# Two stored spectra loaded earlier, the u rows moved to other tables, and the order lists of four engines written anew

## The chip, the cores and the metric

The kernel runs on one core of one Trainium2 chip. The metric is the device time of one execution in microseconds (us), as the median of several. Executions of one kernel here lie within about 3% of each other, and some fall into a slower state with a lower granted clock; those are named. Medians and ranges below are over all executions, ratios over the fast ones alone. The engines are TensorE (PE in the profile), VectorE (DVE), ScalarE (ACT), GpSimd (POOL) and the DMA engines, whose transfers are issued by SyncE (SP), ScalarE and GpSimd.

## The reference, cut to what matters

Two independent parts of 2048 x 448 outputs stand side by side. Part A is a linear attention with softmax features. Part B is a long convolution of a signal u with a kernel K that is itself a sum of 256 damped complex rotations for each of 448 channels:

```python
P = jnp.exp(logdA[:, :, None] * l[None, None, :])             # damped rotations
K = jnp.einsum("dn,dnl,dn->dl", Cc, P, dB).real               # kernel rows, 448 x 2048
Kf, Uf = rfft2(pad(K)), rfft2(pad(u))                         # spectra (calls cut)
y = irfft2(Uf * Kf)[..., :L] + u * Dskip                      # product of spectra, inverse, skip term
out = concatenate([attention(x), y], axis=-1)
```

## The kernel before: what the change touches

K is built in four quarters of the channels. For each quarter ScalarE evaluates two tables, rotations (Sin, lines 487 and 488) and dampings (Exp, line 496, with a negation in line 498). VectorE multiplies them (lines 534 and 535, then 539 to 542), and TensorE multiplies the low table W by the high table U (line 566) into kernel rows:

```python
def rotations(qt):                                   # T: Sin
    p = args(TH, ...)
    for e, n, f, rows_ in evals(2):
        act(T[:, 0, rows_, :], p[:, e:e + n], ACT.Sin, scale=float(f), bias=bias_hp[:, :])   # 487
        act(T[:, 1, rows_, :], p[:, e:e + n], ACT.Sin, scale=float(f))                       # 488
def dampings(qt):                                    # W: Exp
    ...
    act(W[:, c, ...], p[:, e:e + n], ACT.Exp, ...)                                           # 496
    act(W[:, c, 1:30:2, 1, :], W[:, c, 1:30:2, 0, :], ACT.Copy, scale=-1.0)                  # 498
def damp(qt, c):
    yield TT(out=w[:, 1:30:2], in0=w[:, 1:30:2], in1=t[:, 0:N_ABS - 1], op=ALU.mult)         # 534
    yield TT(out=w[:, 0:31:2], ...)                                                          # 535
    ...
```

A copy (line 570) takes the rows out of TensorE's banks, and a scatter (line 672) of 20 small DMAs turns them into the natural order. DFT tiles (line 681) and matmuls (line 696) then make a kernel spectrum for each of three column groups, which ScalarE evicts (line 699). The first group holds two quarters, called group 0 here; groups 1 and 2 are quarters 2 and 3.

```python
def scatter_k(gi, Ts, engs):
    for kt, h0, h1, l0, l1 in K_ROWS:
        for g in range(4):
            next(engs).dma_start(out=Kt[:, kt, ...], in_=Ts[32 * g + h0:32 * g + h1, l0:l1, :])   # 672
def load_su(gi):                                     # stored spectrum of u, from DRAM
    nc.gpsimd.dma_start(out=SU[gi]..., in_=SUd...[:, :, 112 * q0:112 * (q0 + nq)])                # 779
def conv_group(gi, SU, SK, UD, GI, OB):
    prod(...)      # VectorE: SU times SK, line 712; sums in 717 to 727
    inverse(...)   # UD times Dskip (729); TensorE: inverse DFT (738), skip term (740); eviction (745)
```

Nothing is left to a scheduler: four lists fix the order of all instructions of TensorE, ScalarE, VectorE and SyncE.

```python
def in_order(tc):
    for engine, name in (("PE", "PE"), ("ACT", "Activation"), ("DVE", "DVE"), ("SP", "SP")):
        places = ...decode(ORDER[engine])
        for a, b in zip(places, places[1:]):
            tc.add_manual_dep(queues[name][b], queues[name][a].name, info, reason="order")
```

In the program built from this, eight semaphores are shared in turn by the DMAs of SyncE and ScalarE, so that each such DMA waits for the eighth before it.

The softmax here doesn't subtract the row's maximum and nothing guards it: scores larger than these inputs give would overflow.

## Time and profile before

Three runs had a median of 339.19 us (334.77 to 339.36). The profiled execution took 335.67 us; the span between its first and last instruction is 333.9 us.

| stage (us from the start) | VectorE busy | VectorE idle | what ends the longest waits |
|---|---|---|---|
| 0 to 261.3: attention, tables, kernel rows | 233.2 | 28.1 | loads (first 20 us), ScalarE's tables (quarters 1 and 3) |
| 261.3 to 326.1: convolution | 57.0 | 7.8 | group 2's kernel spectrum, 6.2 |
| 326.1 to 333.9: last inverse and stores | 0 | 7.8 | |

The longest wait of the convolution, in VectorE's timeline (start, duration, what, idle before and its releaser):

```profile
312.26 3.96 DVE L712 TENSOR_TENSOR sbuf<-sbuf 128x3584 bf16<-128x3584 bf16 x2 [6.16 <-ACT sbuf L699]
```

The page also draws the span as 40 equal slices (8.35 us each), each digit the busy share of a slice in tenths. Two of its rows, before:

```profile
DVE  4689999899998999949799999999699999995590
DMA  7947000000001111014111213579821848510006
```

VectorE is at 90% and more nearly everywhere. The dips are the first two slices, the "4" and "7" at 142 to 167 us, the "6" at 234 us and the two fives before the end. The DMA engines are busy from 217 to 242 us ("798") and again during the last scatter (from 275 us, "85").

### The profile page before, as it was taken

The numbers are of one execution on the slowest core, as the hardware profiler recorded it, in microseconds if no ns is written. First come the engines' busy times: TensorE is split into PE (matmuls) and PEld (weight loads), VectorE is DVE, ScalarE is ACT, GpSimd is POOL, SyncE is SP. The second block draws the span as 40 slices with busy tenths as digits, with TensorE's granted clock in tenths as the row PEclk, the third lists the DMA queues.
The fourth block names the chain that finished last, engine by engine and source line by source line (L and its number), as shares of the span: only waits on it lengthen the run. The fifth ranks groups of instructions, "written<-read, shape, count | busy, mean of one in ns | idle before, by whom it ended". The sixth has DMA issues, their size and how long they took to land.

```text
span 333.9 us, 8889 instructions
## 1 busy us (share of the span) xinstructions
PE 248.6 (74%) x3735; PEld 180.1 (54%) x3735; DVE 290.2 (87%) x361; ACT 251.8 (75%) x539; POOL 10.3 (3%) x20
## 2 busy tenths in 40 slices
PE   2937858888738778999489987889449853599864
PEld 1914534444425445666256755567338742598854
DVE  4689999899998999949799999999699999995590
ACT  5899999999999999998669996899993310132411
POOL 3000000000000000000000000020000040000000
PEclk9987899999987997999589999999789795599979
DMA  7947000000001111014111213579821848510006
GB/s 218 272 117 224 22 1 0 29 0 27 3 0 69 47 52 57 19 47 129 35 43 57 71 59 75 163 259 306 254 54 31 295 118 155 166 62 2 2 2 220
DMA packets 32055, 31.42 MB, mean 94 GB/s; under 512 B 10448, under 2 KB 30704, under 8 KB 31632
## 3 DMA queue, kind: packets, MB, share of 16 engines
q1 hardware_dynamic: 28856, 25.42, 25.4%
q0 software_dynamic: 1296, 5.15, 5.8%
q8 instruction: 29, 0.48, 0.6%
q10 hardware_dynamic: 1864, 0.30, 0.5%
q14 instruction: 10, 0.08, 0.1%
HBM read 22.94 MB, written 7.34 MB: 91 GB/s over the span
## 4 chain that ended last, share of the span: by engine, by line
DVE 25%; PE 16%; ACT 12%; DMA 7%; issue 3%; SPq 1%; DVEq 0%; ACTq 0%
DMA sbuf<-sbuf 5%; DVE sbuf L540 3%; DVE sbuf L542 3%; ACT sbuf L496 3%; DVE sbuf L539 3%; DVE sbuf L642 3%; DVE sbuf L535 2%; PE bank_72 L696 2%; DVE sbuf L534 2%; DVE sbuf L712 2%; ACT sbuf L699 2%; PE bank_71 L696 2%; PE bank_65 L738 2%; DMA out_dram<-sbuf 2%; PE bank_66 L738 2%
## 5 line engine op out<-in xcount | busy, mean ns | idle before, releaser
L566 PEld LDWEIGHTS <-sbuf 128*16 128x16 bf16 x1792 | 36.9, 115 | 9.7 <-issue 7.5
L318 PE MATMUL bank_72<-sbuf 128*128 128x448 bf16 x128 | 32.7, 379 | 6.9 <-ACT sbuf L321 5.9
L738 PEld LDWEIGHTS <-sbuf 128*128 128x128 bf16 x384 | 28.5, 103 | 14.5 <-issue 13.3
L699 ACT CAST sbuf<-bank_72 128x448 bf16<-128x448 f32 x28 | 15.5, 553 | 27.5 <-DMA sbuf<-sbuf 15.2
L696 PEld LDWEIGHTS <-sbuf 128*128 128x128 bf16 x336 | 24.8, 108 | 20.0 <-issue 18.4
L696 PE MATMUL bank_72<-sbuf 128*128 128x112 bf16 (+1 forms) x256 | 25.3, 249 | 10.8 <-ACT sbuf L699 10.5
L712 DVE TENSOR_TENSOR sbuf<-sbuf 128x3584 bf16<-128x3584 bf16 (+1 forms) x9 | 23.6, 2643 | 6.3 <-ACT sbuf L699 6.2
L566 PE MATMUL bank_65<-sbuf 128*16 128x48 bf16 x896 | 23.0, 262 | 2.2 <-DVE sbuf L542 2.2
L566 PE MATMUL bank_66<-sbuf 128*16 128x48 bf16 x896 | 23.8, 262 | 0.2
L579 PEld LDWEIGHTS <-sbuf 112*128 112x128 bf16 x128 | 12.3, 98 | 19.8 <-issue 11.5
L321 ACT CAST sbuf<-bank_72 128x448 bf16<-128x448 f32 x32 | 18.5, 577 | 4.3 <-PE bank_72 L318 4.2
L534 DVE TENSOR_TENSOR sbuf<-sbuf 128x3360 bf16<-128x3360 bf16 x8 | 15.2, 1903 | 6.7 <-ACT sbuf L488 3.5
L318 PEld LDWEIGHTS <-sbuf 128*128 128x128 bf16 x128 | 12.0, 102 | 16.2 <-issue 10.2
L542 DVE TENSOR_TENSOR sbuf<-sbuf 128x896 bf16<-128x896 bf16 (+1 forms) x24 | 18.7, 779 | 0.7
L539 DVE TENSOR_TENSOR sbuf<-sbuf 128x896 bf16<-128x896 bf16 (+1 forms) x24 | 18.6, 777 | 0.4
L540 DVE TENSOR_TENSOR sbuf<-sbuf 128x896 bf16<-128x896 bf16 (+1 forms) x24 | 18.6, 775 | 0.3
L639 PEld LDWEIGHTS <-sbuf 112*128 112x128 bf16 x128 | 9.3, 102 | 16.5 <-issue 12.7
L496 ACT ACTIVATE sbuf<-bank_67 128x112 bf16<-128x112 f32 (+2 forms) x60 | 18.0, 412 | 0.0
L496 ACT ACTIVATE sbuf<-bank_68 128x112 bf16<-128x112 f32 (+2 forms) x60 | 18.0, 452 | 0.0
L586 DVE TENSOR_REDUCE sbuf<-sbuf 128x32 f32<-128x896 bf16 x16 | 17.3, 1081 | 0.4 <-ACT sbuf L582 0.3
L579 PE MATMUL bank_70<-sbuf 112*128 112x448 bf16 x64 | 14.7, 351 | 3.0 <-ACT sbuf L584 3.0
L522 DVE TENSOR_TENSOR sbuf<-sbuf 128x448 bf16<-128x448 bf16 (+3 forms) x16 | 16.5, 1030 | 0.2
(177 smaller groups left out, 653.0 us busy)
## 6 DMA issues: line engine op xcount, KB each, us to landing
sbuf<-const SPq DMA_DIRECT2D x32, 224.0 KB
SUd<-sbuf SPq DMA_DIRECT2D x16, 224.0 KB
sbuf<-const SPq DMA_DIRECT2D x2, 1024.0 KB
sbuf<-in_A_x_dram SPq DMA_DIRECT2D x4, 448.0 KB
out_dram<-sbuf SPq DMA_DIRECT2D x16, 112.0 KB
sbuf<-SUd POOLq DMA_DIRECT2D x1, 1792.0 KB, 13.3
sbuf<-in_B_u_dram SPq DMA_DIRECT2D x4, 448.0 KB
sbuf<-SUd POOLq DMA_DIRECT2D x2, 896.0 KB, 9.4
```

The source lines that it names most:

```text
L318: mm(p[:, 0:D_MODEL].rearrange("p (q g x) -> p q g x", q=4, g=4), lhsT=G1[:, cp, jt, 128 * mt:128 * mt + 128], rhs=by_quarter(ab[:, cp ^ s ...
L496: act(W[:, c, a:a + 2 * (rows_.stop - 1 - rows_.start) + 1:2 * rows_.step, 1 - neg, :], p[:, e:e + n], ACT.Exp, scale=float(f - 2 * f * neg))
L534: yield TT(out=w[:, 1:30:2], in0=w[:, 1:30:2], in1=t[:, 0:N_ABS - 1], op=ALU.mult)
L539: yield TT(out=t2, in0=flipped(src), in1=far[:, :, cols].unsqueeze(1).to_broadcast([128, n, 2, COLS]), op=ALU.mult)
L540: yield TT(out=dst, in0=src, in1=PW[512][:, 0, cols].unsqueeze(1).unsqueeze(1).to_broadcast([128, n, 2, COLS]), op=ALU.mult)
L542: yield TT(out=dst, in0=dst, in1=t2, op=ALU.add)
L566: mm(p[32 * g:32 * g + N_HI, qq * N_LO:(qq + 1) * N_LO], lhsT=U[qt % 2][:, c, :, ri, xc], rhs=W[:, c, :, ri, xc], start=(i == 0), stop=(i ...
L579: mm(p[:, :], lhsT=xT[:, dj, ts], rhs=w[:, dj, :], start=(dj == 0), stop=(dj == 3))
L696: mm(p[:, k2, :].rearrange("p (q g x) -> p q g x", q=nq, g=4), lhsT=f_tiles[i][1][:, fi, :], rhs=natural(Kt[:, kt, :] if kt < 5 else K0[:, ...
L699: nc.scalar.copy(SK[:, b, i0 // 8, i0 // 4 % 2, i0 % 4:i0 % 4 + per, :], p[:, :, :])
L712: TT(out=T[:, i], in0=su.unsqueeze(1).to_broadcast([128, 2, 2, n8]), in1=sk.unsqueeze(2).to_broadcast([128, 2, 2, n8]), op=ALU.mult)
L738: mm(p[:, k2, :], lhsT=GI[r][:, cp, mt, 128 * jt:128 * jt + 128], rhs=S[:, r, cp, mt, :], start=(cp == 0 and mt == 0), stop=False)
```

## The change

Its intent is to take two 896 KB loads away from the last scatter, and to let the kernel spectrum of the last group be ready before VectorE asks for it. The stored spectra of groups 1 and 2 (the change calls them column groups 2 and 3) go into the high table that quarter 2 leaves free. For that the u rows of the skip term go to the low tables, and the second inverse matrix and the output buffer move within them.

```diff
-    SU = [group_tile("SU", i, at) for i, at in enumerate((oL, oW + 22528, oW + 29696))]
+    SU = [group_tile("SU", i, at) for i, at in enumerate((oL, oU, oU + 7168))]
-    GI = [sb(f"GI{r}", [128, 2, 4, 512], BF16, (oL + 21504, oW)[r]) for r in range(2)]
-    UD = sb("UD", [128, 2, 2, 4, D_MODEL], BF16, oU)
-    OB = sb("OB", [128, 2, 2, 4, D_MODEL], BF16, oW + 8192)
+    GI = [sb(f"GI{r}", [128, 2, 4, 512], BF16, (oL + 21504, oW + 28672)[r]) for r in range(2)]
+    UD = sb("UD", [128, 2, 2, 4, D_MODEL], BF16, oW)
+    OB = sb("OB", [128, 2, 2, 4, D_MODEL], BF16, oW + 14336)
@@ rank 70000
-                (the four loads of UD)
                 kernel_spectrum(0, SK[0], list(range(16)), RING)
                 load_su(0)
                 nc.gpsimd.dma_start(out=GI[0][:, :, :, :], in_=GI_d[0])
+                load_su(1)
+                load_su(2)
@@ rank 80000
+    (the four loads of UD)
     nc.sync.dma_start(out=GI[1][:, :, :, :], in_=GI_d[1])
-    load_su(1)
-    load_su(2)
@@ ORDER
-    "PE": ..., "ACT": ..., "DVE": ..., "SP": ...
+    "PE": ..., "ACT": ..., "DVE": ..., "SP": ...      (all four anew)
```

More of the change, by code (lines that the diff above doesn't have):

```diff
@@ L101 @@
     "PE":
-        'c-q}qKWGzC7{5OWQbgp23?dGPgwmlyhaw_HL^>1+(xH?fMKWXv5+s922ZsznGGquMQlvwW3?iWfCx;t~h-B#CkfB2;89F#fDUzW!x${D'
-        'Quk?Mq^PPD)6XX%T`~LsA?|tv(bWO*K1KvNUoUI*?=iegy&xC);|J@0&ahK2=I*)I-JpRGgTP8Xd!Qa64I-$S!=?8ee?mwG&9>Rf-Zva'
-        '1m{zt%LA6^CT$bWuJ<Yox|7Vrt7v$&oTdIosS<KxW&&ieFcL}v|n)8l2Uz&C++FXV7>Ef9Xs<Lxg>^b?v`uLxMvcs;6b6F#+*1#~2GNe'
-        'O=ia8Kjk)uALF8t)vl5B!Rxem3BD;+M%$f7gJwiC-PKrHkY0>HJ<xxZ-$zK<)<FPhFjlr$hb!<zjKP`sgE5%x7`!Lhc^q9N;NaobM;XX'
-        'L%+xvHWXRzX9e6(Q6HO`F+$U7vP`f!Bz!vC1X6jeR>A-W;Auq!Eaetv!}XNy=d(hC47hEzvQa<tLx%^tq;`fri_5TR<yf`d>ba|4<c9f'
@@ L107 @@
-        '#C<fcSg!`D*NPi$KhS=!O8k9O?9VdlTI#FWVe_Yp_iY<|e{J`ptsC=y-p>+$bEcZVJ@{D;n9mK=Vb$RKhwZa$z<#NLUp9Dp0rZR!@_c}'
-        'Nj`+W=*uMqEemgM(&TGXv(P8Hh><$#|?ZV!Yq>t=~&mUXU|LfI8e{LzxheN#gOl&;&4>m{QgUQy1?bk1g_aL_4DlzfANK5jxpkIpdbz='
-        'Y19NY)D0_^9(FOa!rlX=GE>H&5#;BS*S(nOD~wNri$Mzt*1?-F|c7v`}s;e96PpPLciWp?26p`xExg4nZ)HebMI(Vg!3xFE>=t0ZPiV)'
-        'HU={#4BUNI;uWydUfXCKc@zCHnJ!n5XXuzCOnPfTf80C52d<6Yg6pWX(De$I&A_9-r{{1jikH-;Z<ENE~TJf8~&QWh2fjPvWTP(>>p1D'
-        '>34XelEFhJc#JK7X5z6?sYGR--5h<Q?uDHb0<VBNeTZTgpJ`@T=(T3$=>sraz7riUmOX4am07m3|Y&m+jnEK(+XL)X{*m~=?zl{',
@@ L112 @@
-    "ACT":
-        'c-nPS&r6h16g_VSvk?~=Xg_8`a>$ub(KJmGBB*tniYVG76jqCHBN4UgKPUpDA%YfdT(k;m(XNtySfNExWJN|~iy(9`a!%*n@6GTvV|=`'
-        'O&wcmY`_9}q&%q&~RVVwK4$k6)*<WmwZ9tI;q{MLe$tKwaMvMrN9<N3{O7vAdcxgK&u2BbPxh1B=TMGT1xOIvbxf9bQm)VOM`EJ=R)y;'
-        '5$L)KwZ6%qQxHn_?+$+gG@tv>reac3-lU-7nBd{^;+d{SJ$?kFCL<#*vCcgwoicYzMo-xqF@?Z;l6;(nn$I%$FjV~kro0<Za@&KZ<-xX'
-        'Comi=VdqIXnt|ci?eA1&-rc)oE9>SH{tdhj|9IigMaNYiJAJSM~VD0X*S)!x=Q=2b&Fl=en9cNhu%1KA{)t(j$MHM_H6#Ry@YTE1X@f^'
-        '!MHlKZgmS1NgwKP%pAVQ|v<<X8%!^!CaM6udR&dI1>BS9$ivynuk_A{RWSjh61nRGW{K27aFlOY>a+9Wr4@BT{FJM6X?T~oi)yrL4Sw1'
-        'r-i!YNAZW9cx#MyybG$bXu&*ND*vW#Y^bQsROT?tR{49(;koJ>{yVWWzAC>Ft@vye4j;L>hV_OWc+I>ahplGwF=c+`HGBWMl6DIvuF`G'
-        '2lDcSmjq>F;S08RNDPNRN8D~CZo5G8aCjJ+XL;Z~',
@@ L120 @@
-    "DVE":
-        'c-mD`TT22#7(KJD(iTC{MYM~F5xsPQUVG`ef89^Ws3=Or2Q$lrpfu6bnc2~u<zx1nIp3V~U1nn#OldG<f(U=wS&L+wAPd3jk&Ikq%6WX'
-        'q4Sl~jzx&D5M;LJ*#@kqEf>$;ch{3lqtp?{OUVEQm4X^qVV0EY73Xnb3LUsbAif(Y)!iQ95eys^P4)Pk@F;=9c6-&wPYvNb&raWczxs8'
-        'Fk>?^|shHSapv75uPy0kp2ThD2BITm`Ty4tLx!<1oAk!nT0==dX5X{TOW@N6edP3zp<d*-h)@8X?h?QLxbnqooh9rXNL6#P8qHKi8rFL'
-        'RaM=;jq}d4?uWaj(+}9>hJuqf=<O*$$YhtOPn)w)SFL;nb{O_dP`Zn{^fCs<5^s`{BgBl;xAf96Qn9XuXXYWzH*?FmY%a%l=A(f1V!J{'
-        '{',
+        'c-qxiJ!o1{6!txzEmBI6@`el<92`rLBAGgLaBv7kN`_J#GDvYKMM?*U5*$jW3=R$%q&S4q!6AeW4jDozC4+QwaLC}`;8a4%U=!c#3;nM'
@@ new lines @@
+        '3p5EuZdf!9k5U%IkbIv{Io}YX2jEDh<VI8?V&fpQjyB^=A%gbyLp6~9z-x;z;p^3HN&gMJv_Q&4ez~JdcXSUoS<aUXljDF+q&3Xs>Pl^'
+        '0T@W+8O-(L{EPaeHM&R{Z(en9BYu{J<25k3a5u+|8j$zKq9lF&DR_ki2L`@ox6Yf~|v2AlZK{7d<qqbgs-dZMUjhw!V~(<6M3vG#oKFH'
+        'P=;#cN3PF#R#$!^nJbnA9BBgdw))(%@^;cEtV<L61lI{iH+k(&Y7bu6emdp$9z|(4Y0WUv^$P%KP;V^dzbA1hJR#x51w!{@On0(i-;TY'
+        'd~+xBE9bl^&A!V%A>K~{iWe&M^ldsQaI<_)zicL?}lvex<kVd-y3~%^G-15(0ndA%k@7IvVPVtXkB+Ce%mB2bqW6yO*_Xl{xbW}XZobR'
+        'Hc-Fu-{L;ia(TZ00CJnRg6#t_XSM4vx#E2y=TpBYn)h1PjBl6D+{ni~@~Z`W2l!o|ceM$=g30I20qA8@ELX>ViOB5}xyc*?ds}#~-y5_'
@@ new lines @@
+        '2>k~N!pCMl}!o6Qzh@nr6uERZN6!6?oy%N8V^FkK&(Kf>MzveTCR^Z1wOH9vzo*{M2^0#V<^_C&OZ}IP2h0v*7k>#x=o>Li|E_rSnko&'
+        'aZ-*~*-K7J_3qi0Kg+jM(OdCh0&dx*(T%{crL^&`!@J!g5j<aeMcpnWCyR){t>B>TIvejteLea)W!13DjS>NytJmethRaQN?T>k0|QoZ'
+        '8mBFZ%!47fpQ+6nn|3<~d16JfHg3iM!hI&PT$1i=vYKmx^=CTl4R?hsuI;&Yn4Y{|(Xm!Bm@#a|&m-C3?2W{=l7YW@6u<&t%^u6?1VjG'
+        'M_yYJ0$xVcQL&k#TZu=^t}$KZt4NmweEXy+p}XdHFNJt`0arFKU4HSw_^S74<a2u4*',
+    "ACT":
+        'c-nnaOK(k46#n)-+-gdddW95iN<CWSURrURFfnFELWCL+Gb8?h0n<{6NY%uMiAY2w1`@YXkEShJue8x3BnBcuTlajvz0SF(?G4S&+Iu~'
+        '}wb$BfJ2<37bF~*(U>PP!&cSb1NJDyCg)E*Qmt`S-uu?jQaXLGHGG+Ek!wH$efGh=i%;=o2*pL(EpF)5?@=i;amba7Kgnn+7tzXg>i*7'
+        '=Moo7zeCT>XD=ggu3Z^W&~TSI%z4RCP<As=y366x0i$r<<z(LL@<Zi)SUWp{Ycq`PdLhO!5z*^X}R(mfxtJV6VP)jnzWaOh$czKdMR`o'
+        'a|ne-`IC#u}W#1&;Cvn(-v=S=KQ8+J-(B@i*ax_)DS=RT))UTy-URhUhTcT8Yp6D4&b$!tzA>iK|NdhFOpI?BN09dw34Fxep7NmsB^So'
+        'AcN`OTKk@r)<4EthpHGGj5k|EpBp$&NcWT<QA;PC?9htYA_~W-{GnFW%Au^+!B0?Yg>$5NtTn`jK)N|!9&w*0XlgZ?QF(%9@RUa;xTEj'
+        'u>((q*U96OGP>baX?iWg6`nveae+-@qfL~<ROfU5tvA3e`RvC%^Q^^7{g=J!!3b+H^3S*VO8*W^;rm^mXp0l<@Jh8s$bIyEADDr%Q8XB'
+        '98Z53gp6WckHB=3Qikr|+OT*U_vf8Rjq0F*JzckR~d#c7S*~(G;mwI1mz0Kh-2YVTg',
@@ new lines @@
+    "DVE":
+        'c-mD`Yfr*J5S(5QXcLX1K+z8-hDbsJ>SzD|FA$&6M3g8BC`2Vh4PEE%3S4{X?d{`cccxVcA$(Gap|FsJl<-Giql$^_AjsC6)a|a3GOJj'
+        '-OMl7=kq@bIH#lQSFr@b)2lm!L_O1PqVHR=gTQ)uKTuwZ%D*-y5zsFvtqw}6*opIRDt4KYY@^uxdVI&p2bGDQ*gHa|{YlUEtFD;uE?qt'
+        'q6x^j#Q>EMb?6^`&AGkTA#`6SmVZHNeSt3!waG|Wj`6}P>q1B_)NP4uX21AVgZ$suP=c`8!j5|mx;wmFTcYl2D+V<0AaN=6C^D{4elMA'
+        'K+fHBD{IOs4l1zNBxbD)NmotFsPgIn*V`YfjU~4fVJscZC>D+|xG5+NtBF)12G%cPw51bsz1qDChb(eM8#R?m_NLx>evmXYw1Edl^#~<'
+        '5!mVRfgo=h?yC0xG!ot``G`T3F7$',
@@ L126 @@
     "SP":
-        'c-lo!yN<#@44fq)AOZ*p5E2rUk?8piI=+)1xRzf43MeTk?i$4FE+NC%<b*7H?b%s-ya7R02U+v%j{zlzxbTfcusT(p=(L)Q<&m=!<ox&'
-        'oD@DU&=hkG#zVpE)zW9$%apc6^@_@ClK5m*g!&WiZo77)Fm|@Q=+nW2U+XF9bV(yxDRi|(Ek@*H!b`{U;xrTrZEvD$=#Ex#B>Rkvc*pl'
-        '9Yb!7voGuGI9Mi}9TrSIN=u@k8<J-M)E^&9lRh~!CC#|Xab3;7O;Vg',
+        'c-lQs%MJlS5Ukl<k4<pkA`&8T;p7vX{jP6tadUMbB90=25c^Q7o0!d1PpYeSx+WkX0-31384Gh(g-zU5b7x96k<nJcx@+nD_e&hjHOIo'
+        'e#+kaJKNi9SGc1`i;KH`L1031^@1B^IdL7(^6YP0qOa6={8@RHDF*ck^wdF}Q#hNdsQdBj0ggy=&`4pC8$Ka=-aL33`<Wc&EPxMlP2n8'
@@ L130 @@
+        ')gtj^@;J9|D$6>I8%E{rjy-SU(xlOuKQ`{$*nEoq+bTYLZ&4T5I',
 }
@@ L824 @@
             with rank(70000):
-                for b in range(2):
-                    for r in range(2):
-                        nc.sync.dma_start(out=UD[:, b, r, :, :], in_=rows(u2, b, r, 0))
                 for i in range(8):
@@ L832 @@
                 nc.gpsimd.dma_start(out=GI[0][:, :, :, :], in_=GI_d[0])
+                load_su(1)
+                load_su(2)
                 kernel_spectrum(1, SK[1], [*range(8, 16), *range(8)], RING)
     tc.cur_priority = 80000
+    for b in range(2):
+        for r in range(2):
+            nc.sync.dma_start(out=UD[:, b, r, :, :], in_=rows(u2, b, r, 0))
     for i in range(4):
```

## The prediction

> **What bounds the kernel now.** I cut the span into five stretches where the work changes: preparation and the key side of the attention (0 to 100 us), query side and the first two quarters of the table building (to 200), the last two quarters (to 261.3, where the first convolution product starts), the convolution of group 0 and most of group 1 (to 306.1), and the rest. The view of busy time by stretch, columns named in its first line:
>
> ```profile
> core 0: us, PE busy (x) PEld busy (x) DVE busy (x) ACT busy (x) POOL busy (x), PEclk, DMA share, GB/s
> 0.00:100.00 100.00, 68.98 (x547) 43.15 (x548) 86.33 (x129) 94.92 (x168) 4.68 (x16) 0.94 0.28 76
> 100.00:200.00 100.00, 84.10 (x1411) 55.55 (x1411) 89.70 (x124) 91.43 (x219) 0.00 (x0) 0.91 0.18 57
> 200.00:261.30 61.30, 46.02 (x947) 35.17 (x946) 57.17 (x67) 49.09 (x116) 2.28 (x2) 0.94 0.57 166
> 261.30:306.10 44.80, 30.94 (x495) 28.13 (x495) 43.37 (x31) 10.06 (x27) 3.36 (x2) 0.77 0.50 134
> 306.10:333.90 27.80, 18.52 (x342) 18.09 (x338) 13.64 (x15) 6.24 (x13) 0.00 (x0) 0.93 0.20 68
> ```
>
> Until 200 us VectorE and ScalarE are both near full; after 261.3 VectorE alone is, until 306.1. VectorE has 86.33 + 89.70 + 57.17 = 233.2 us of work before 261.3, so 28.1 us of idling; of the convolution it has 43.37 + 13.64 = 57.0 us, done between 261.3 and 326.1, so 7.8 us of idling. No instruction is removed by the change, so a gain can only come out of these two sums or out of the tail after VectorE's last instruction (326.1 to 333.9).
>
> Next, where the idling sits. From the timeline of VectorE (start, duration, what, idle before and its releaser), the two long waits before 261.3:
>
> ```profile
> 150.08 1.91 DVE L534 TENSOR_TENSOR sbuf<-sbuf 128x3360 bf16<-128x3360 bf16 x1 [3.18 <-ACT sbuf L498]
> ...
> 239.79 1.91 DVE L534 TENSOR_TENSOR sbuf<-sbuf 128x3360 bf16<-128x3360 bf16 x1 [3.10 <-ACT sbuf L488]
> ```
>
> Both are the first damping product of a quarter (1 and 3), both wait for ScalarE's tables. With 1.29 us just before the first of them, also for ScalarE, that is 7.6 of the 28.1 us. About 8.4 lie in the first 20 us (loads), 1.7 at 164 us behind a load of u rows, the rest in crumbs.
>
> The chain of waits (start, duration, what) for the last part:
>
> ```profile
> 269.85 0.53 ACT sbuf L570
> 270.39 0.63 SPq L672
> 271.08 0.99 SPq L672
> 272.11 11.20 DMA sbuf<-sbuf
> ...
> 308.52 0.98 PE bank_71 L696 x20
> 310.68 1.00 PE bank_71 L696 x20
> 311.70 0.54 ACT sbuf L699
> 312.26 3.96 DVE sbuf L712 x2
> ```
>
> The scatter of the last quarter's kernel rows (line 672) costs 15 us on it, then group 2's kernel spectrum (lines 696, 699) is finished so late that VectorE's first product of group 2 (line 712) starts at 312.26. The view of waits puts 6.2 us on that product. Why the scatter is slow shows in the timeline of all engines:
>
> ```profile
> 270.36 3.36 POOL L779 DMA_DIRECT2D sbuf<-SUd  x2 [47.65 <-ACT sbuf L570]
> 270.39 15.52 SPq L672 DMA_DIRECT2D sbuf<-sbuf  x10
> ...
> 271.00 15.59 ACTq L672 DMA_DIRECT2D sbuf<-sbuf  x10
> ```
>
> The two loads of stored spectra that the change moves (line 779, 896 KB each, rows of 224 bytes) are issued in the same instant as the 20 scatter DMAs. Two queues need 15.5 us for ten each, 1.55 us apiece. The 20 scatter DMAs of quarter 2 went out from one queue between 236.1 and 249.4 at a median of 0.597 us each.
>
> **What the Trainium skill says.** "DMA: Bandwidth & Descriptors", section Issuing engines are not separate DMA queues: transfers from all queues run on the same 16 engines and interleave, and a second issuer saves issue time only. The trace agrees: two issuers were slower here than one had been. Same page, Specifications: below 512 bytes per transfer the line rate is not reached. The scatter (56-byte rows) and the spectra (224-byte rows) are both below; the u rows (896 bytes) are not, so the u loads that take the spectra's place late in the kernel are the better kind. "ScalarE: Activation LUTs", What ACT_TABLE_LOAD costs: 1283 ns for the load plus about 1380 ns of drain. The trace shows 1.28 us for a load (at 217.14) and the next activation at 218.43, so I count 1.28 us per switch and no drain.
>
> **The change part by part.**
>
> Buffers. The u rows of the skip term move to the lower half of the low table (W), the spectra of groups 2 and 3 to the high table of even quarters, and the second inverse matrix and the output buffer move inside W. In the order of the changed program the spectra loads wait only for the table products of quarter 2, so they are issued around 227 to 236 us instead of 270.4. The u loads wait for the first half of quarter 3's table products (ending at 258.7 in the trace of before), and they stand before the last scatter on their queue. What is then in front of or beside the scatter is the inverse matrix, 1 MB, which must now wait for all table products (269.7) instead of half of them; an estimate from the 5.5 us to landing of its sister load is that it delays the scatter by 3 us. The scatter alone, at 0.6 us per issue on two queues, needs some 6 to 7 us, but in the new order ScalarE's half of it also waits in turn for the late DFT tiles. I expect it to land 4 to 6 us earlier relative to the last table product. By itself that is worth nothing: VectorE has 43 us of other convolution work at that time.
>
> Skip rows. VectorE's two multiplications with u (line 729, 3.95 us together) moved from second and third place of the convolution to sixth and eighth. Five instructions stand before the first of them, 3.9 + 1.1 + 1.1 + 3.9 + 1.1 = 11 us; the loads are issued about 2.5 us before the convolution starts, so they have 13 us for 1.8 MB, where 1.8 MB of worse rows took 13.3 us in a busy stretch. I take this wait as at most 1 us.
>
> TensorE's order. This is the part I pay for. Before, 56 of group 2's 112 spectrum matmuls stand behind most of the inverse matmuls of group 0 and of group 1's first half. After, all 112 stand ahead of them. Then VectorE's wait of 6.2 us before group 2, and the 1.05 us wait at 304.9 for TensorE to release a buffer, should both go: 7.3 us at most. The spectrum needs the scatter landed (about 22 to 25 us after the convolution starts) and some 10 us more; VectorE reaches group 2 after 43 us. So the slack is 8 us or more. I credit 5.5 us, because the new order has waits of its own for TensorE's release of the shared product buffers.
>
> ScalarE's order. Table loads fall from 29 to 27, 2 x 1.28 = 2.6 us. I also added up, with durations from the trace, the work standing ahead of the tables that VectorE waits for: for quarter 1's 143 us before and 137 after; for the last rotations of quarter 3, 224 and 219. So the tables should come 5 to 6 us earlier if ScalarE's own waiting stays as it is. VectorE's work ahead of those products is unchanged (130 and 212 us), as is that ahead of the first convolution product (233). Of the 7.6 us of such waiting I credit 5 us, since the order is new everywhere and will have some waits that I can't see.
>
> Sum: convolution start 261.3 - 5 = 256.3; plus 57.0 of VectorE's work and 2.3 of waits, 315.6; plus the tail of 7.8, 323.4 of span instead of 333.9, that is 10.5 us less. The profiled execution of before took 335.67 us, so 325.2. Two of three plain runs of before took 339, so I add 2: 327 us.
>
> **Rivals.** (1) The wait only moves: VectorE then waits for u rows or for the shared buffers, and the front stays at 261 because a new order brings as many waits as it removes. For it: VectorE waits for TensorE to release a product buffer in five places of the new order, and the order of before was surely chosen with care too and still left 28 us. Then about 333 to 337 us. (2) Contention moves forward: the spectra now fall into 220 to 250 us, where the DMA share is already 0.96 (220 to 240) and the DFT tiles for group 0's spectrum are loaded between pieces of a scatter. If group 0's spectrum is late, the first product is late, and the front gains nothing; the end still gains 5: about 331. Against: the u loads leave just this stretch, with the same bytes. (3) Everything fits: all 7.6 and 7.3 us and some crumbs are gained: about 319.
>
> **Range and chances.** The middle case is 327; rival 3 sets the lower edge, 319.5, rival 1 the upper, 334.5. Before should average about 338 again, so faster by over 2% means below 331. Rivals 1 and 2 have about a quarter together: 0.73 faster, 0.23 the same, 0.04 slower.
>
> **What would show it.** Right: VectorE's first product of line 712 near 256 us; no wait over 1 us before the group 2 products; the spectra loads issued before 240; the last scatter shorter than 15 us; VectorE's span from first product to last instruction near 59 us instead of 64.8. Wrong: the waits for lines 498 and 488 are back at the same length, line 729 waits for u, or the first product waits for line 699.

## The result, and the profile after

The changed kernel took 325.27 us (median of 4 runs, 323.29 to 328.01), the one before 338.6 us in the same rounds (4 runs, 334.77 to 339.36), all fast. The ratio is 0.964, with a 95% interval from 0.9559 to 0.9721. Such ratios are the mean time of one kernel's fast runs over that of the other's fast runs of the same rounds, so not quite the ratio of the medians. The predicted 327.0 us and the range 319.5 to 334.5 held, and so did "faster by over 2%".

The same two rows of the page, after (slices of 8.07 us):

```profile
DVE  4489889989999999999999989999679899999990
DMA  7955200000000111011402122657972059450024
```

The dip at 150 us and the two fives at the end are gone. The one near 234 us is still there, and it is deeper (the "6" and "7"). The busy DMA time has moved forward, but the slices of the scatter are not empty ("9" at 266 us, "5" at 282).

Busy time by stretch, cut where VectorE's first convolution product starts and where its last instruction ends:

```profile
core 0: us, PE busy (x) PEld busy (x) DVE busy (x) ACT busy (x) POOL busy (x), PEclk, DMA share, GB/s
0.00:257.76 257.76, 197.89 (x2755) 132.34 (x2755) 231.66 (x318) 230.20 (x492) 10.33 (x20) 0.89 0.31 88
257.76:315.10 57.34, 46.55 (x930) 43.32 (x919) 56.65 (x44) 17.91 (x43) 0.00 (x0) 1.00 0.41 131
315.10:322.80 7.70, 3.22 (x66) 3.05 (x63) 0.00 (x0) 1.06 (x2) 0.00 (x0) 0.97 0.44 150
```

Against the table of before the front is 3.5 us shorter (261.3 to 257.8), the convolution 7.5 us (64.8 to 57.3), the tail 0.1 us: together 11.1 us. In the convolution VectorE now idles 0.7 us in all. The medians differ by more, 13.3 us: the profiled execution of before (335.67 us) is among its faster ones. The convolution's 57.3 us came back within 0.1 us in a second profile of the changed kernel (run changed_again below); the front did not, where it was 259.35 us, so that only 2.0 of the 3.5 us are seen in both.

VectorE's timeline (start, duration, what, idle before and its releaser) at the places that the prediction looked at:

```profile
145.62 1.90 DVE L534 TENSOR_TENSOR sbuf<-sbuf 128x3360 bf16<-128x3360 bf16 x1
...
235.65 1.91 DVE L534 TENSOR_TENSOR sbuf<-sbuf 128x3360 bf16<-128x3360 bf16 x1 [4.59 <-ACT sbuf L488]
...
257.76 3.89 DVE L712 TENSOR_TENSOR sbuf<-sbuf 128x7168 bf16<-128x7168 bf16 x1 [0.71 <-ACT sbuf L699]
...
268.50 2.02 DVE L729 TENSOR_TENSOR sbuf<-sbuf 128x3584 bf16<-128x3584 bf16 x1
...
300.69 3.96 DVE L712 TENSOR_TENSOR sbuf<-sbuf 128x3584 bf16<-128x3584 bf16 x2
```

Quarter 1 (145.62) has no wait any more. Quarter 3 waits 4.59 us instead of 3.10. The multiplication with u does not wait, and neither do the products of group 2, which had waited 6.2 us.

The transfers, from the timeline of all engines:

```profile
222.64 1.69 POOL L779 DMA_DIRECT2D sbuf<-SUd  x1
...
232.63 1.68 POOL L779 DMA_DIRECT2D sbuf<-SUd  x1 [8.29 <-PE bank_66 L566]
...
271.46 7.36 SPq L672 DMA_DIRECT2D sbuf<-sbuf  x10
...
279.18 3.07 ACTq L672 DMA_DIRECT2D sbuf<-sbuf  x3
...
284.44 5.39 ACTq L672 DMA_DIRECT2D sbuf<-sbuf  x7
```

The spectra leave 39 and 48 us earlier. SyncE's half of the scatter now takes 0.74 us apiece instead of 1.55; but before, two queues took turns, so that the 20 DMAs together went out at 0.81 us apiece (16.2 us). ScalarE's half now does not start until 279.18 and pauses in the middle, so that the 20 take 18.4 us. The chain of waits shows why, and when the scatter has landed:

```profile
270.96 6.06 DMA sbuf<-const
...
280.76 3.65 DMA sbuf<-const
284.42 0.02 issue
284.44 0.60 ACTq L672
...
287.65 2.78 DMA sbuf<-sbuf
290.43 0.09 issue
290.52 0.63 PE bank_72 L696 x8
```

The 1 MB inverse matrix (270.96) and a DFT tile (280.76) stand in front of pieces of the scatter, and the piece for which TensorE waits lands at 290.4 us. That is 19 us after the last table eviction has ended (271.4). Before, TensorE's last wait for the scatter ended at 287.9, which is 17.5 us after it (270.4).

### The profile page after: what moved, and what is told of

Read it like the earlier page. It is cut to its first block, busy times and chain, and to the rows that moved or that the text cites.

```text
span 322.8 us, 8872 instructions
## 1 busy us (share of the span) xinstructions
PE 247.7 (77%) x3735; PEld 178.7 (55%) x3735; DVE 288.3 (89%) x361; ACT 249.2 (77%) x537; POOL 10.3 (3%) x20
## 4 chain that ended last, share of the span: by engine, by line
ACT 18%; DVE 14%; PE 13%; DMA 5%; issue 2%; SPq 2%; ACTq 1%; DVEq 0%
PE bank_72 L696 5%; ACT sbuf L496 4%; DMA sbuf<-const 3%; DVE sbuf L712 2%; ACT sbuf L615 2%; DVE sbuf L642 2%; ACT sbuf L498 2%; ACT sbuf L487 2%; DMA sbuf<-sbuf 2%; PE bank_66 L566 2%; PE bank_65 L566 2%; ACT sbuf L699 2%; ACT L496 2%; ACT sbuf L488 1%; SPq L672 1%
## 5 line engine op out<-in xcount | busy, mean ns | idle before, releaser
L566 PEld LDWEIGHTS <-sbuf 128*16 128x16 bf16 x1792 | 37.3, 115 | 22.0 <-issue 13.3
L696 PE MATMUL bank_72<-sbuf 128*128 128x112 bf16 (+1 forms) x256 | 28.2, 262 | 7.7 <-ACT sbuf L699 6.4
L696 PEld LDWEIGHTS <-sbuf 128*128 128x128 bf16 x336 | 24.5, 105 | 14.3 <-issue 10.4
L318 PE MATMUL bank_72<-sbuf 128*128 128x448 bf16 x128 | 30.9, 363 | 1.8 <-ACT sbuf L321 1.7
L738 PEld LDWEIGHTS <-sbuf 128*128 128x128 bf16 x384 | 26.6, 97 | 8.2 <-issue 8.1
L566 PE MATMUL bank_66<-sbuf 128*16 128x48 bf16 x896 | 23.8, 263 | 0.0
L579 PEld LDWEIGHTS <-sbuf 112*128 112x128 bf16 x128 | 12.6, 101 | 17.9 <-issue 9.9
L318 PEld LDWEIGHTS <-sbuf 128*128 128x128 bf16 x128 | 11.9, 99 | 10.8 <-issue 3.7
L579 PE MATMUL bank_70<-sbuf 112*128 112x448 bf16 x64 | 15.5, 365 | 2.5 <-ACT sbuf L584 2.4
L522 DVE TENSOR_TENSOR sbuf<-sbuf 128x448 bf16<-128x448 bf16 (+3 forms) x16 | 16.5, 1029 | 0.2
L523 DVE TENSOR_TENSOR sbuf<-sbuf 128x448 bf16<-128x448 bf16 (+3 forms) x16 | 16.4, 1023 | 0.3
```

The costliest lines, as they stand in the source:

```text
L318: mm(p[:, 0:D_MODEL].rearrange("p (q g x) -> p q g x", q=4, g=4), lhsT=G1[:, cp, jt, 128 * mt:128 * mt + 128], rhs=by_quarter(ab[:, cp ^ s ...
L566: mm(p[32 * g:32 * g + N_HI, qq * N_LO:(qq + 1) * N_LO], lhsT=U[qt % 2][:, c, :, ri, xc], rhs=W[:, c, :, ri, xc], start=(i == 0), stop=(i ...
L579: mm(p[:, :], lhsT=xT[:, dj, ts], rhs=w[:, dj, :], start=(dj == 0), stop=(dj == 3))
L696: mm(p[:, k2, :].rearrange("p (q g x) -> p q g x", q=nq, g=4), lhsT=f_tiles[i][1][:, fi, :], rhs=natural(Kt[:, kt, :] if kt < 5 else K0[:, ...
L738: mm(p[:, k2, :], lhsT=GI[r][:, cp, mt, 128 * jt:128 * jt + 128], rhs=S[:, r, cp, mt, :], start=(cp == 0 and mt == 0), stop=False)
```

## The experiments

Twelve runs were made; two of them repeat a kernel. All gave correct results. Where only an order list was changed, the edit is told as the order of the instructions. In two runs (new_buf_old_order and new_tail_on_old) the written list is a line shorter, so that line numbers are one lower (711 for 712). Numbers such as "first product" are from the profile of each run.

**Does the order or do the buffers carry it?** Two crossings: the new buffers with the old lists of TensorE, ScalarE and VectorE, and the reverse.

```diff
 # new_buf_old_order: changed kernel, its SyncE list
-"PE", "ACT", "DVE": lists of the changed kernel
+"PE", "ACT", "DVE": lists of the kernel before
 # old_buf_new_order: kernel before, its SyncE list
-"PE", "ACT", "DVE": lists of the kernel before
+"PE", "ACT", "DVE": lists of the changed kernel
```

> The new buffers and DMA order with the old order lists of TensorE, ScalarE and VectorE. Order theory (the gain is the order's, the buffers only make it possible): VectorE's old order asks for the u rows second in the convolution, and they now land late, so it waits about 5 us there; group 2's spectrum is late as before; 336 to 342 us. Buffer theory (early spectra and a free scatter make the gain): the scatter lands some 8 us earlier and the time is 326 to 330 us.

> The old buffers and DMA order with the new order lists of TensorE, ScalarE and VectorE. Order theory: the front keeps its 3.5 us and TensorE's order its gain, but the scatter meets the spectra loads again, and group 2's spectrum had only 0.9 us to spare in the changed kernel, so VectorE waits 3 to 8 us in the convolution: 328 to 333 us. Buffer theory: nothing is left of the gain, 335 to 339 us.

Measured: 348.58 us (345.97 to 349.6, and one slow run of 352.58) and 343.79 us (342.85 to 347.56), ratios 1.0234 (interval from 1.0158 to 1.031) and 1.0139 (from 1.0064 to 1.0215). Both are slower than either kernel, and both theories missed the time. The first product started at 275.2 and 272.0 us, 17 and 14 us later than in the changed kernel. The lists of the three engines and the order of SyncE's DMAs are a matched set: in the second crossing, for example, VectorE waits 4.0, 3.5, 1.7 and 1.9 us for attention matmuls in the front, and in the first 16.5 us before quarter 3. So crossings cannot apportion the front. Two readings survive. The profile of the first fell in the slow state, so only waits are read from it that have the length of before:

```profile
150.73 1.91 DVE L533 TENSOR_TENSOR sbuf<-sbuf 128x3360 bf16<-128x3360 bf16 x1 [3.21 <-ACT sbuf L497]
...
291.03 11.98 SPq L671 DMA_DIRECT2D sbuf<-sbuf  x10
...
291.63 9.17 ACTq L671 DMA_DIRECT2D sbuf<-sbuf  x10
...
329.18 3.96 DVE L711 TENSOR_TENSOR sbuf<-sbuf 128x3584 bf16<-128x3584 bf16 x2 [6.16 <-ACT sbuf L698]
```

The first crossing has the old lists, and it shows the two waits of quarter 1 again (1.29 and 3.21 us). The second has the new lists and no wait before quarter 1's first damping product. Quarter 1's waits follow the lists and not the buffers. And in the first crossing the early spectra leave the scatter alone (12 us for its 20 DMAs, 16.2 before), yet VectorE waits the same 6.16 us before group 2. With the old lists the early spectra are worth nothing there, as the order theory says ("late as before").

**The order of the convolution alone.**

```diff
 # new_tail_on_old: kernel before; only group 2's spectrum and the inverse work reordered
-TensorE: 56 of group 2's 112 spectrum matmuls behind all inverse matmuls of group 0 and 47 of group 1
+TensorE: spectrum, inverse and skip matmuls (696, 738, 740) in the changed kernel's order
+ScalarE: their evictions (699, 745) in the changed kernel's order
```

> The kernel before, with only the convolution part of TensorE's and ScalarE's order (group 2's spectrum, inverse matmuls, their evictions) taken from the changed kernel. If TensorE's order is what made VectorE wait 6.2 us before group 2, the wait shrinks to 0 to 3 us and the time is 331 to 335 us. If the late scatter is the cause, nothing changes: 336 to 339 us.

Measured: 331.98 us (three fast runs, 331.75 to 332.06, and one slow), ratio 0.9769 with an interval from 0.9712 to 0.9826. The lines of its timelines:

```profile
273.25 14.49 SPq L671 DMA_DIRECT2D sbuf<-sbuf  x10
...
273.92 15.44 ACTq L671 DMA_DIRECT2D sbuf<-sbuf  x10
...
306.03 3.95 DVE L711 TENSOR_TENSOR sbuf<-sbuf 128x3584 bf16<-128x3584 bf16 x2
...
321.91 0.63 DVE L726 TENSOR_TENSOR sbuf<-sbuf 128x896 bf16<-128x896 bf16 x1 [2.62 <-PE bank L739]
```

The scatter is as slow as before, and yet group 2 does not wait. VectorE's convolution went from 262.27 to 322.53 us, 60.3 us instead of 64.8. So the order alone is worth 4.6 us, and a new wait of 2.6 us near the end is what it does not win. TensorE's clock is no rival here, though it differs between the two kernels (mean granted clock of the convolution 0.82 before, 1.00 after): this run had 0.86 and no wait, and the repeat of the changed kernel had 0.94 and the same 57.3 us as with 1.00.

**The early spectra alone, taken away.**

```diff
 # spectra_late: changed kernel
-                load_su(1)
-                load_su(2)
@@ behind the load of GI[1]
+    for gi in (1, 2):
+        nc.gpsimd.tensor_copy(SU[gi][0:16, 0, 0, 0, 0, 0:1], Ts[0:16, 0, 27:28])   # waits for the last kernel rows
+        load_su(gi)
```

> The changed kernel, with the two spectra loads held back until the last eviction of the kernel rows, when the old kernel issued them. If their contention with the scatter counts: the scatter lands 4 to 8 us later, group 2's spectrum (0.9 us to spare) is late by about as much, 328 to 333 us. If the early loads are worth nothing by themselves: 324 to 327 us as the changed kernel.

Measured: 333.06 us (three fast runs from 329.2 to 333.24 and one slow of 334.2), ratio 0.9765 with an interval from 0.9683 to 0.9847. All four lie above the ten executions of the changed kernel (323.29 to 328.01). The first product started at 257.84 as in the changed kernel, but VectorE's convolution took 61.9 us instead of 57.3.

```profile
270.38 8.60 SPq L672 DMA_DIRECT2D sbuf<-sbuf  x10
...
271.58 3.37 POOL L779 DMA_DIRECT2D sbuf<-SUd  x2
...
288.34 5.60 ACTq L672 DMA_DIRECT2D sbuf<-sbuf  x7
...
294.63 3.55 PE L696 MATMUL bank<-sbuf 128*128 128x112 bf16 x36 [4.64 <-DMA sbuf<-sbuf]
...
305.27 3.96 DVE L712 TENSOR_TENSOR sbuf<-sbuf 128x3584 bf16<-128x3584 bf16 x2 [2.92 <-issue]
```

With the loads beside it, ScalarE's half of the scatter ends 4 us later. TensorE waits 4.64 us for it, and group 2's products wait 2.9 us; 1.4 us before group 1 are most of the rest. The early spectra are worth 4.5 us of convolution here. The profiled execution is the fastest of the four (329.2 us); the median is 7.8 us above that of the changed kernel, and the traces account for 4.5. The two parts overlap: 4.6 us for the order alone and 2.9 us more for everything else (60.3 to 57.3), or 3.0 for everything but the early spectra (64.8 to 61.9) and 4.5 for them (from the times before rounding, 64.82, 60.26, 61.85 and 57.34). Not tested is whether the spectra would still matter if ScalarE's half of the scatter went out at once: no run holds them back with that order.

**The scatter issued at once.** This and the next three ran against 338.93 us of before.

```diff
 # scatter_at_once: changed kernel, ScalarE's list
 two evictions 570 (the last kernel rows)
+ten scatter DMAs 672
 eviction 699 of group 1, four evictions 745, ...
-three, then seven scatter DMAs 672
```

> The changed kernel with one part of ScalarE's order moved: its ten scatter transfers of the last quarter stand directly behind its last table eviction (line 570) instead of behind a spectrum eviction of group 1 and four result evictions. Theory (VectorE bounds the convolution in the changed kernel, the 0.9 us of slack before group 2 is just enough): ScalarE's half begins near 272 instead of 279 us, the last piece lands 5 to 8 us earlier (282 to 285), the last eviction of group 2's spectrum ends several us before VectorE's first product of group 2, and the time stays within 1 us: 324 to 327. Rival (the slack is used up in some executions, so the scatter is still on the path): 1 to 3 us faster, 322 to 324. Rival (ScalarE, held in its queue by the semaphores that the scatter shares with the 1 MB inverse matrix, evicts group 1's spectrum late): slower, 328 to 332, with a wait of VectorE before group 1.

Measured: 324.86 us (324.27 to 326.12), ratio 0.959. The time is as the first theory said, but its picture of the scatter was wrong (the last piece was to land by 282 to 285 us):

```profile
271.99 7.28 ACTq L672 DMA_DIRECT2D sbuf<-sbuf  x10
...
279.91 6.70 SPq L672 DMA_DIRECT2D sbuf<-sbuf  x10
...
300.63 0.53 ACT L699 CAST sbuf<-bank 128x448 bf16<-128x448 f32 x1 [0.45 <-PE bank L696]
```

ScalarE's half starts at 271.99, and SyncE's half, which had started at 271.46, now starts at 279.91. The halves share semaphores, so only their turn was swapped. The last issue ended at 286.6 instead of 289.8. Group 2's last eviction (300.63) came no earlier than in the changed kernel (299.25), because its matmuls stand in TensorE's list behind inverse matmuls that wait for VectorE. In this profile the chain of waits from 277 to 303 us consists of VectorE's own instructions; the scatter is off it. That makes VectorE the bound of the convolution, with or without the scatter's order.

**ScalarE's table swaps before quarter 3.**

```diff
 # fewer_tables: changed kernel, ScalarE's list
 ..., 496
+496 (the single one)
 table load, 487, 488, 487, 699, 570, 488
-table load, 496 (the single one)
 699
-table load
 487, 699, 488, ...
 # tables_and_evictions: as above, and
+two evictions 570
 table load, thirteen 496, 498
-two evictions 570
 # all_three: both, and scatter_at_once
```

> The changed kernel with one ScalarE instruction moved: the single table instruction of line 496 that stands at 229.57 us between two activation table loads goes behind another of its kind at 224.20, so that 25 table loads are left of 27 (2 x 1.28 = 2.6 us). Theory (quarter 3's wait of 4.59 us comes from ScalarE's own table swaps): that wait falls to about 2.0 us and the first convolution product starts 1.5 to 2.6 us earlier, 255.2 to 256.3; time 322.5 to 324. Rival (that wait is hidden behind the evictions of group 0's spectrum, which already hold the first product by 0.71 us): the wait of quarter 3 gets shorter, the wait before the first product grows by as much, and the time moves by less than 1 us.

> As the run before (two table loads fewer), and besides ScalarE's two evictions of line 570 at 223.46 us stand before the 13 instructions of line 496 and not behind them. Theory (TensorE's wait of 7.27 us for these evictions delays group 0's spectrum, which then holds the first product): TensorE's wait shrinks to about 1.5 us, group 0's spectrum is done 2 to 5 us earlier, and what the fewer table loads win reaches the first product: start 254.5 to 256, time 321.5 to 323.5, 0 to 2 us under the run before. Rival (VectorE's own work and ScalarE's tables set the start): no difference to the run before beyond 0.7 us.

> All three edits of ScalarE's order together: two table loads fewer, the two evictions of line 570 first, the ten scatter transfers at once. Theory (the gain at the front moves the whole convolution up, including the last table product and the scatter, and the earlier scatter keeps the slack for group 2): as the run before or up to 1 us better, 320.5 to 323.5, and group 2's products without a wait. Rival (ScalarE blocked by the transfers): slower than the run before by 1 to 5 us.

Measured: 322.93 (321.23 to 325.58), 324.75 (322.06 to 326.26) and 324.49 us (323.37 to 325.77), ratios 0.9532, 0.9576 and 0.9576. All intervals overlap each other and that of the changed kernel. The second and third miss the gain that was expected of them; the first has the time that its theory gave, but not the picture: quarter 3 waits 4.00 us and not 2.0, and the first product starts at 258.74 and not by 256.3, in a profile that is the slowest of its six executions. I compare the profiles by the stretch from the end of quarter 2's last damping product (line 535) to the start of quarter 3's first (line 534), which does not depend on what came before. It was 23.7 us in the changed kernel, 23.1 with fewer tables, 22.5 with the evictions moved too and 23.8 with all three. Two profiles of one kernel differ by as much as these: the changed kernel had 23.7 and 24.2, fewer_tables 23.1 and 22.9. Two table loads fewer are 2.6 us of ScalarE's time; 0.6 us arrived, hardly more than that spread. In the run with fewer tables ScalarE then waits 1.22 and 0.40 us for TensorE before evictions of line 699 in that stretch, where it had not waited before. Part of the freed time turned into a wait for the next engine.

**The control, and all tables of one kind together.** Before 339.54 us.

```diff
 # changed_again: no edit
 # tables_once: changed kernel, ScalarE's list between 217 and 239 us
+two evictions 570, all 487 and 488 (evictions 699, 570 between them as they were)
+table load, all 496, 498
-487/488, load, 496 x13, 498, 570 x2, 496, load, 487/488, load, 496, load, 487/488, load
```

> The changed kernel once more, as the control for the run beside it. By all theories 324 to 326.5 us, the first convolution product at 257 to 258.7, quarter 3's wait for ScalarE at 4 to 4.7 us.

> The changed kernel with ScalarE's order redone in one place: between 217 and 239 us all instructions of lines 487 and 488 stand first, then all of lines 496 and 498, and the two evictions of line 570 ahead of both; 23 activation table loads in the kernel instead of 27 (4 x 1.28 = 5.1 us, of which 3 x 1.28 = 3.8 us before quarter 3's first damping product). Theory (quarter 3's wait comes from the length of ScalarE's work between the last damping product of quarter 2 and the first of quarter 3, 23.7 us in the changed kernel against 21.6 before, because of the table swaps that the new order put there): that stretch falls to 20 to 21 us, the wait from 4.6 to at most 1.5 us, and the first convolution product starts 2 to 3.5 us earlier if the evictions of group 0's spectrum move up with it: 254 to 256, time 321 to 323.5. Rival (the evictions of group 0's spectrum, paced by TensorE and by the DFT tiles, hold the first product): the wait of quarter 3 goes, a wait of 2 us or more for line 699 stands before the first product, and the time is that of the control within 1 us.

Measured: 324.68 us (324.4 to 326.45) and 326.77 us (325.86 to 327.16), ratios 0.9587 and 0.9628. The control repeats the time, and the convolution (57.3 us). It does not repeat the front as closely: the first product came at 259.35 us and quarter 3 waited 5.08 us, both outside what was expected. So a difference of a microsecond or two in the front between two profiles is not to be read as the edit's. With four table loads fewer the kernel is not faster, and quarter 3's first product comes 27.3 us after quarter 2's last instead of 24.2:

```profile
224.56 0.53 ACT L699 CAST sbuf<-bank 128x448 bf16<-128x448 f32 x1 [5.23 <-PE bank L696]
...
232.43 1.28 ACT L496 ACT_TABLE_LOAD   x1
```

Both the theory and its rival missed: an eviction in the middle of the table work was not yet ready, and ScalarE stood 5.2 us behind it.

**The same, without that wait; and the best list once more.** Before 340.05 us.

```diff
 # tables_once_no_idle: as tables_once, but
+all 487 and 488 without a break, then 699, 570, 699, 699
+table load, thirteen 496, 498, then the late 570, two 496
 # fewer_tables_again: as fewer_tables
```

> As tables_once (23 activation table loads instead of 27), which had lost its gain because two spectrum evictions of group 0 stood in the middle of ScalarE's table work and TensorE was not ready for them (5.2 us idle, then crumbs). Here the instructions of lines 487 and 488 run without a break, the evictions stand behind them, and the one eviction of line 570 that TensorE finishes late stands behind the work of lines 496 and 498. Theory (length of ScalarE's work between the quarters sets the start): ScalarE's stretch from the table load near 211.6 us to the end of line 498 is 24.0 - 3.8 = 20 to 21 us, quarter 3's first damping product starts near 232.5 and its wait is under 2 us; the first convolution product starts 2 to 3.5 us earlier than in the changed kernel, 254 to 256, time 321 to 323.5. Rival (group 0's spectrum, evicted later here, holds the first product): a wait of 2 us or more for line 699 before it, time 324 to 327.

> The best of the ScalarE orders so far (322.93 us) once more, on another chip and beside the run above. If its gain over the changed kernel (324.68 to 325.27 us) is real: 322 to 324 us and a ratio below 0.957. If it was chance: 324 to 326 and a ratio of 0.957 to 0.962.

Measured: 324.3 us (321.14 to 325.51) and 323.67 us (322.54 to 325.34), ratios 0.9532 and 0.953. In the first, quarter 3 starts 23.3 us after quarter 2's last product and waits 4.19 us: ScalarE now waits 0.83, 1.78 and 0.77 us before three evictions of group 0's spectrum. TensorE, before them, had waited 1.17 us for a scatter DMA and 3.09 us for VectorE. The rival's mark, a wait of 2 us or more before the first product, is missing too: there is none. The theory of the table swaps is thus mostly refuted: swaps fill ScalarE's time there, but behind them stands TensorE's spectrum work at nearly the same length.

The version with fewer tables had 322.93 and 323.67 us, the changed kernel 325.27 and 324.68. They were run at other times. Over 12 and 10 runs the means are 323.4 and 325.3 us. Its repeat met the mark set for a real gain (322 to 324 us, a ratio below 0.957), so it is probably faster than the changed kernel, by 0.6%. But the intervals overlap, and the kernel that has the same edit and one more (324.75 us) does not support it; so I do not call it shown.

Two more kernels stopped in the builder with a deadlock: the changed kernel with the old convolution order of TensorE and ScalarE, and one that was to delay ScalarE's quarter 1 tables behind other work.

## Why the prediction was right, step by step

- **The sum.** Predicted 256.3 + 59.3 + 7.8 = 323.4 us of span; measured 257.8 + 57.3 + 7.7 = 322.8. The total is as near as that by luck, because two errors cancel: the front was credited 1.5 us too much, the convolution 2 us too little.
- **TensorE's order removes the wait before group 2.** Right, and shown alone: 60.3 us against 64.8 with nothing else changed. The reading of the lists was off in one point: not all inverse matmuls of group 0 now stand behind the spectrum. In the traces 95 of its 128 run before group 2's first spectrum matmul (15 before the change), while the scatter is still under way. What moved forward is the second half of the spectrum: it had begun at 308.36 us, behind all 128 and 47 of group 1's, and now begins at 295.12, behind 110 of group 0's alone. I had withheld 1.8 of 7.3 us for new waits; the whole kernel won 7.5.
- **"By itself that is worth nothing", of the early spectra.** Wrong for the changed kernel: taken away they cost 4.5 us. The step that failed is the slack of "8 us or more", and in it the landing of the scatter, put at 22 to 25 us after the convolution starts. It came 32.7 us after (290.4 less 257.8). The other two terms held: the spectrum needed 8.4 us more where 10 had been allowed, and VectorE came after 42.9 us where 43 had been said. (In the program, group 2's first product reads the half whose last eviction is the last but one; it ends at 298.79 us, and VectorE comes at 300.69.) So the slack was 1.9 us, and a delay of the scatter by 4 us more than uses that up. For the old lists the sentence holds: in the first crossing the spectra left early too, and the wait before group 2 stayed.
- **The scatter lands "4 to 6 us earlier".** Wrong: 1.5 us later relative to the last table eviction. I had seen that the inverse matrix and DFT tiles stand between its pieces, but put only 3 us on the matrix. It took 6.06 us (270.96 to 277.02), and a tile 3.65 us more. The pace was misread as well: 1.55 us apiece is the pace of each of two queues, 0.597 us the duration of one issue. Counted alike, the last scatter went out at 0.81 us apiece and quarter 2's, 20 in 13.9 us, at 0.7. Nor are two issuers the slower by themselves: without the spectra the two queues of the first crossing sent 20 in 12.0 us (a slow-state profile), the two in turn of scatter_at_once in 14.6. The contention is real all the same, but it sits in the landing: on the chain a scatter DMA took 11.20 us to land beside the spectra before the change (272.11), and 2.78 us without them after it (287.65).
- **Quarter 1's waits go.** Right: 1.29 + 3.18 us were there before, none after, and VectorE starts quarter 1 at 145.62 instead of 150.08.
- **Quarter 3's wait goes.** Wrong: 3.10 became 4.59 us. The step that failed is the addition of the two waits. The tables did come earlier, by 4.1 us where 5 to 6 had been said: the last rotation that the product needs ended at 239.76 us before and 235.61 after. But VectorE came to them 5.6 us earlier (231.06 instead of 236.69), because quarter 1's wait and 1.69 us for u rows at 164 us were gone. And the program lets ScalarE overwrite the rotations only after quarter 2's last damping product (line 535), so the start of its work moves with VectorE. Counted from that product the stretch is 23.7 us (211.91 to 235.65) against 21.6 before (218.17 to 239.79). Of the 4.5 us won at quarter 1, 4.1 are left at quarter 3 and 3.6 at the first product, where 0.71 us for group 0's last evictions now stand.
- **Skip rows.** The cost (at most 1 us) was right: no wait. The loads went out at 260.67, about 3 us after the convolution had started and not 2.5 before it; VectorE needed them 7.8 us later, and that was enough.
- **Table loads.** Right: 27 instead of 29, at 1.28 us each. ScalarE's busy time fell from 251.8 to 249.2 us, which is the 2.6 predicted. What it does for the time is little, as the experiments on swaps show.
- **Rivals.** "The wait only moves" was true of quarter 3 and of nothing else. "Contention moves forward" cost at most the 0.71 us at the first product. Open is what the front could still give: VectorE idles 26 us there, 10.1 of it in the first 20 us, where it was 8.4 before.

## What to carry to other kernels

Before calling a transfer's speed worthless, work out when it lands with everything that stands in front of it on the semaphores it shares, and count its slack from there to the instruction that needs it; two changes that each remove the same wait overlap, so test each alone and each taken away. For an engine that may only start after another has released a buffer, compare the stretch from that release, and not the work from the start of the kernel. Two waits of one engine for another do not add up: once the first is gone, the engine comes earlier to the second. And time taken out of one engine can come back as its wait for the next, as it did in part here.

## What the Trainium skill lacked or had wrong

- "DMA: Bandwidth & Descriptors", section Issuing engines are not separate DMA queues, speaks of shared engines and of issue time. No page says that the issue order of two queues is coupled when their DMAs share semaphores, as in this program: moving ScalarE's ten DMAs from 279.2 to 272.0 us moved SyncE's ten from 271.5 to 279.9 us.
- The same page gives no cost for small rows beside other small rows. Here a scatter DMA of 56-byte rows took 11.20 us to land beside loads of 224-byte rows, and another 2.78 us without them; ten of them on SyncE's queue took 8.60 us to issue beside those loads (spectra_late) and 7.36 us without.
- "ScalarE: Activation LUTs", section What ACT_TABLE_LOAD costs: the 1283 ns are what every load here shows (1.28 us), but the drain of about 1380 ns is not to be seen. In the changed kernel the instruction before it ends at 211.59, the load runs from 211.61 to 212.89, and the next activation starts at 212.90.
